# W1 kept even tiles first, weight scales and two norm roots moved from VectorE to GpSimd, and a pooling step put later, in a fused attention and MLP kernel

## The chip, the core and the metric

The kernel runs on one core of one Trainium2 chip. The metric is the device time of one execution in microseconds (us). TensorE is called PE in the profile, VectorE DVE, ScalarE ACT, GpSimd POOL, and SyncE, which issues the DMAs here, SP.

## The reference, cut to what is computed

Inputs are q, k and v of 4 batches, 8 heads, 576 positions and 64 channels, and the weights of two blocks of width 512.

```python
# attention, for each batch and head
q_d, k_d, v_d = mean over groups of 4 positions        # 144 positions
out_up    = repeat(softmax(q_d k_d^T / 8) v_d, 4)
out_local = softmax(q k^T / 8 where |i - j| < 4) v
x = out_up + out_local, heads side by side             # (4, 576, 512)
# first block
u  = x + real(fft over channels (fft over positions (x)))
un = (u - mean(u)) / sqrt(var(u) + 1e-6)               # over the 512 channels
x  = u + relu(un @ w_ch1) @ w_ch2                      # 512 -> 2048 -> 512
# second block
gate = sigmoid(causal convolution of x with 5 taps for each channel)
out  = (gate * (x @ w_val)) @ w_out
```

The weights arrive as 64-bit floats, read by the kernel as pairs of 32-bit words.

## The kernel before

**Layout.** Channels lie on the 128 partitions in 4 groups, positions along the free axis. The MLP is done in 12 units (b, j): batch b, 192 positions j. Unit (0, 0) runs in f32 with the weights as they come (`steps32`). All other units run in pairs of f16 numbers: each weight and each activation is split into a high half and a low half (`hh` and `hl`, `uh` and `ul`), and three f16 matmuls (high high, high low, low high) make a product.

**A unit on PE.** `h_group(g)`, g from 0 to 7, makes 256 of the 2048 hidden channels from W1, into one of two PSUM buffers called `ph`; ScalarE reads it out with a ReLU (`h` in the f32 unit, `hh` in the others) and, in the f16 units, VectorE makes `hl`. `c_group(g)` multiplies these by tile 8 + g of W2 into two PSUM accumulators `pc`. In the f16 units the order is h0, h1, c0, h2, c1, h3 and so on.

**The weights' way.** W1 has tiles 0 to 7 and W2 has tiles 8 to 15, each 128 x 1024.

- `load_w` brings the raw words by DMA into slots that are used several times. W2 has more tiles than slots, so a later tile's load waits until VectorE has read the earlier tile out of the slot.
- `word_w` (through `to_f32`) makes f32 numbers out of the words with three VectorE operations a tile: one tensor_scalar and two scalar_tensor_tensor of 128 x 1024.
- `sumsq_w` sums squares on PE (`gram`); `trace_w` (VectorE, then `tot` on PE) makes one number of it; `pow2` makes of this a power of two, the scale `s_w`, and its inverse, with one-column operations on VectorE.
- `conv_w` splits a tile: ScalarE writes the high half with the scale applied, VectorE the low half. The halves of a tile are written where the f32 numbers of the tile before it lay, and so the tiles are split one after another, and only when the f32 unit no longer reads what they overwrite.

Group g of `steps32` reads the even W1 tiles for g under 4 and the odd ones from there on. In the kernel before, the tiles lie and are split in the order 0, 1, 2, and so on.

**The norm.** `ln(b, j)` makes `uh` and `ul` of a unit: mean, square, sum on PE (`st`), then an inverse square root by an integer first guess and two Newton steps on tiles of 128 x 192 (`vv`, `r`), all on VectorE. For (0, 0) the root is used only at the end of the unit.

**The second batch.** Its banded attention, its pooled attention (`pool_qk` sums q and k over 4 positions into `qkT`) and its FFT run between the matmuls of the first batch's units. The value and output weights (tiles 16 to 19, `raw`) follow W2 into slots that the second batch's v gives free, and `pooled_v` on GpSimd sums v, whose loads share SP's queue with those of the weights.

**What sets the order.** The program is written as steps with positions (`put`, `spread`; constants such as `S_W1`, `S_C1`), some raised by `urgent`. A scheduler orders the instructions of each engine from these; on the chip each engine takes its instructions strictly in that order, and waits for the semaphores of each.

Of the kernel before, what the change touches and what calls it, by code (L numbers as in the profile page):

```python
# [126 lines left out]
def attn_moe_kernel(ctx, tc, q_t, k_t, v_t, w1, w2, w_val, conv_t, w_out, c_feat, c_seq, c_band, c_eye, out):  # L127
# [38 lines left out]
    def mul(eng, out, a, b):  # L166
        return eng.tensor_tensor(out=out, in0=a, in1=b, op=ALU.mult)
# [67 lines left out]

    def pow2(f2, kexp, name):

        s = keep.tile([P, 1], F32, name="s_" + name)
        iv = keep.tile([P, 1], F32, name="iv_" + name)
        c = tiny.tile([P, 1], F32, tag="p2a", name="p2a")  # L240
        V.tensor_scalar(out=c, in0=f2, scalar1=1e-30, scalar2=1e30, op0=ALU.max, op1=ALU.min)
        e = tiny.tile([P, 1], I32, tag="p2b", name="p2b")
        V.tensor_scalar(out=e, in0=c.bitcast(I32), scalar1=23, scalar2=None, op0=ALU.logical_shift_right)
        m = tiny.tile([P, 1], I32, tag="p2c", name="p2c")
        V.tensor_scalar(out=m, in0=e, scalar1=-1.0, scalar2=float(2 * kexp + 127), op0=ALU.mult, op1=ALU.add)
        h = tiny.tile([P, 1], I32, tag="p2d", name="p2d")
        V.tensor_scalar(out=h, in0=m, scalar1=1, scalar2=None, op0=ALU.arith_shift_right)
        for dst, sg in ((s, 1.0), (iv, -1.0)):
            b = tiny.tile([P, 1], I32, tag="p2e", name="p2e")
            V.tensor_scalar(out=b, in0=h, scalar1=sg, scalar2=127.0, op0=ALU.mult, op1=ALU.add)  # L250
            V.tensor_scalar(out=dst.bitcast(I32), in0=b, scalar1=23, scalar2=None, op0=ALU.logical_shift_left)
        return s, iv

    def total(cols, n, name):

        ps = pst("tot", [P, n])
        T.matmul(out=ps, lhsT=ones, rhs=cols, start=True, stop=True)
        t = keep.tile([P, 1], F32, name="f2_" + name)
# [18 lines left out]
    def hi(i):  # L277
        return halves[i].bitcast(F16)[:, 0:1024]

    def lo(i):  # L280
        return halves[i].bitcast(F16)[:, 1024:2048]

# [25 lines left out]
    def load_w(i):  # L308
        slot = SLOTS[W1_ORDER.index(i) if i < 8 else i]
# [13 lines left out]

    def word_w(i):
        if i < 16:
            raw = raws.pop(i)
            n = 1024 // len(raw)
            pos = W1_ORDER.index(i) if i < 8 else 8
            for z, x in enumerate(raw):
                last = to_f32(W[i + 1].bitcast(I32)[:, z * n:(z + 1) * n], x,  # L330
                       lambda g=gates if pos < 4 else gates1 if pos < 6 else gates2: g.pop(0) if len(g) > 1 else g[0])
            if pos == 7:
                gates2[:] = [last.ins]
                st[0]["worded"] = last
            return
# [9 lines left out]
    def sumsq_w(i, key, first, last):  # L345

        if first:
            gram[key] = pst("cv", [P, P]) if key == "wo" else ps_c.tile([P, P], F32, tag="c1", name="gram")
        x = W[i + 1].bitcast(BF16).rearrange("p (n t) -> p n t", t=2)
        for c in range(8):  # L350
# [11 lines left out]
    def trace_w(key):  # L362
        return total(diagonal(gram[key], key), 1, key)

    def conv_w(i, s, eng):

        h_, l_, r_ = hi(i), lo(i), W[i + 1]
        A.activation(out=h_, in_=r_, func=AF.Copy, scale=s[:, 0:1])
# [6 lines left out]
    def w1_scale():  # L375
        f = trace_w("w1")
        sc["f1"] = f
        sc["s1"], sc["iv1"] = pow2(f, 10, "w1")

    def w2_scale():  # L380
        f = trace_w("w2")
        sc["f2"] = f
        sc["s2"], sc["iv2"] = pow2(f, 14, "w2")
        iv12 = keep.tile([P, 1], F32, name="iv12")
# [585 lines left out]
    def ln(b, j):  # L970
# [22 lines left out]
        if head:  # L993
# [7 lines left out]
        vv = tiny.tile([P, UT], F32, tag="r2", name="vv", bufs=2)  # L1001
        V.tensor_scalar(out=vv, in0=ps, scalar1=1e-6, scalar2=None, op0=ALU.add)
        r0 = keep.tile([P, UT], F32, name="r00") if head else tiny.tile([P, UT], F32, tag="r0", name="r0", bufs=2)
        V.tensor_scalar(out=r0.bitcast(I32), in0=vv.bitcast(I32), scalar1=1, scalar2=None, op0=ALU.logical_shift_right)
        V.tensor_scalar(out=r0.bitcast(I32), in0=r0.bitcast(I32), scalar1=-1.0, scalar2=float(0x5F1FFFF9),
                        op0=ALU.mult, op1=ALU.add)
        r1 = tiny.tile([P, UT], F32, tag="r1", name="r1", bufs=2)
        for a, c in ((-0.703952253, 0.703952253 * 2.38924456), (-0.5, 1.5)):
            mul(V, r1, r0, r0)
            stt(V, r1, r1, a, vv, ALU.mult, ALU.mult)  # L1010
            stt(V, r0, r1, c, r0, ALU.add, ALU.mult)
        r1 = r0
# [30 lines left out]
    def steps32():  # L1043
# [4 lines left out]
        def h_group(g):  # L1048
# [383 lines left out]
```

## Time and profile before

| | us |
|---|---|
| median of 3 runs | 738.41 (735.47 to 739.21) |
| the profiled execution | 738.74 |
| its span, first to last instruction | 736.9 |
| PE busy in the span | 687.7 |
| DVE busy | 476.8 |
| ACT busy | 315.6 |
| POOL busy | 109.9 |

The span is the part of the execution between its first and its last instruction, and all times of the trace below count from its start. Busy time is no share of useful work: a matmul counts as busy at either level of PE's clock, which the profile gives as a granted share of full speed.

### The profile page before, as it was taken

The numbers are of one execution on the slowest core, as the hardware profiler recorded it, in microseconds if no ns is written. First come the engines' busy times: TensorE is split into PE (matmuls) and PEld (weight loads), VectorE is DVE, ScalarE is ACT, GpSimd is POOL, SyncE is SP. The second block draws the span as 40 slices with busy tenths as digits, with TensorE's granted clock in tenths as the row PEclk, the third lists the DMA queues.
The fourth block names the chain that finished last, engine by engine and source line by source line (L and its number), as shares of the span: only waits on it lengthen the run. The fifth ranks groups of instructions, "written<-read, shape, count | busy, mean of one in ns | idle before, by whom it ended". The sixth has DMA issues, their size and how long they took to land. (4 is left out here: it accounts for less than half of the span.)

```text
span 736.9 us, 18501 instructions
## 1 busy us (share of the span) xinstructions
PE 687.7 (93%) x7849; PEld 599.5 (81%) x7849; DVE 476.8 (65%) x1066; ACT 315.6 (43%) x976; POOL 109.9 (15%) x141
## 2 busy tenths in 40 slices
PE   8588799787999998899999999999999999999997
PEld 4245599676888987868898899788989989999895
DVE  4785699688897957465967823838745572642324
ACT  1674212577453536655433636654323131221213
POOL 0400000116222022420303106003010010000000
PEclk9758999996999999999999999999999999999999
DMA  9965207523323301240220001002100000000001
GB/s 237 373 224 179 87 1 265 118 81 106 117 81 102 104 2 38 66 142 3 90 88 2 16 24 42 16 2 76 38 15 16 2 11 20 2 16 1 30 2 44
DMA packets 27575, 53.02 MB, mean 72 GB/s; under 512 B 2112, under 2 KB 16320, under 8 KB 26468
## 3 DMA queue, kind: packets, MB, share of 16 engines
q1 hardware_dynamic: 27492, 51.84, 21.9%
q8 instruction: 61, 1.00, 0.6%
q14 instruction: 22, 0.18, 0.1%
HBM read 45.34 MB, written 8.26 MB: 73 GB/s over the span
## 5 line engine op out<-in xcount | busy, mean ns | idle before, releaser
L1094 PE MATMUL ph<-uh,W 128*128 128x192 f16 x1408 | 197.1, 248 | 0.0
L1094 PEld LDWEIGHTS <-W 128*128 128x128 f16 x2112 | 177.5, 99 | 5.6 <-issue 3.4
L1094 PE MATMUL ph<-ul,W 128*128 128x192 f16 x704 | 174.6, 248 | 0.2 <-DVE ul L1021 0.2
L1114 PE MATMUL pc<-hh,W 128*128 128x192 f16 x1232 | 170.7, 246 | 0.0
L1114 PEld LDWEIGHTS <-W 128*128 128x128 f16 x1848 | 153.3, 98 | 5.8 <-issue 4.3
L1114 PE MATMUL pc<-hl,W 128*128 128x192 f16 x616 | 150.9, 246 | 0.6 <-DVE hl L164 0.6
L164 DVE SCALAR_TENSOR_TENSOR hl<-ph,hh 128x384 f16<-128x384 f32 x88 | 48.4, 551 | 88.8 <-ACT hh L1098 88.8
L1098 ACT ACTIVATE hh<-ph 128x384 f16<-128x384 f32 x88 | 43.1, 490 | 94.0 <-PE ph L1094 91.1
L164 DVE SCALAR_TENSOR_TENSOR W<-X,cw,W 128x192 f32<-128x192 f32 x160 | 63.6, 453 | 1.9 <-ACT W L1169 1.7
L1206 PE MATMUL val<-yy,W 128*128 128x192 f16 x576 | 53.5, 246 | 2.5 <-DVE yy L164 1.3
L1206 PEld LDWEIGHTS <-W 128*128 128x128 f16 x576 | 47.9, 98 | 4.9 <-issue 2.9
L561 ACT ACTIVATE dP<-dS,dmx 128x64 f32<-128x64 f32 x160 | 47.9, 334 | 1.3 <-PE dPT L582 0.9
L1222 PE MATMUL out<-W,gh 128*128 128x512 f16 x144 | 45.6, 379 | 0.0
L561 ACT ACTIVATION_READ_ACCUMULATOR dP<-dS,dmx 128x1 f32 x160 | 36.5, 228 | 0.0
L711 ACT ACTIVATE E<-sc,nm 72x144 f32<-72x144 f32 x64 | 23.6, 380 | 13.7 <-PE po L747 7.1
L1114 PEld LDWEIGHTS <-Wz 128*128 128x128 f16 x264 | 23.4, 102 | 7.5 <-issue 4.0
L164 DVE SCALAR_TENSOR_TENSOR W<-W,W 128x1024 int32<-128x1024 int32 x24 | 28.6, 1216 | 0.0
L170 POOL TENSOR_TENSOR vr<-v 72x256 f32<-72x256 f32 x12 | 16.0, 1336 | 82.5 <-DMA v<-in_v_dram 79.7
L1222 PE MATMUL out<-W,gl 128*128 128x512 f16 x72 | 27.3, 379 | 0.0
L1114 PE MATMUL pc<-hh,Wz 128*128 128x192 f16 x176 | 26.4, 255 | 0.0
L1114 PE MATMUL pc<-hl,Wz 128*128 128x192 f16 x88 | 21.7, 256 | 3.6 <-DVE hl L164 3.6
L1222 PEld LDWEIGHTS <-gh 128*128 128x128 f16 x144 | 14.0, 98 | 13.5 <-issue 0.2
(241 smaller groups left out, 1213.3 us busy)
## 6 DMA issues: line engine op xcount, KB each, us to landing
W<-in_moe_w_ch_dram SPq DMA_DIRECT2D x12, 1024.0 KB
v<-in_v_dram SPq DMA_DIRECT2D x32, 144.0 KB
out_dram<-osb SPq DMA_DIRECT2D x17, 256.0 KB
vw<-in_v_dram SPq DMA_DIRECT2D x16, 256.0 KB
X<-in_q_dram SPq DMA_DIRECT2D x6, 576.0 KB
kT<-in_k_dram SPq DMA_DIRECT2D x4, 582.0 KB
X<-in_moe_w_ch_dram SPq DMA_DIRECT2D x2, 1024.0 KB
raw<-in_moe_w_ch_dram SPq DMA_DIRECT2D x4, 512.0 KB
```

Of the source, the lines that this page charges most:

```text
L164: return eng.scalar_tensor_tensor(out=out, in0=in0, scalar=scalar, in1=in1, op0=op0, op1=op1)
L170: return eng.tensor_tensor(out=out, in0=a, in1=b, op=ALU.add)
L561: A.activation(out=s_[:, z, a], in_=pss[par][:, z, a], func=AF.Exp, scale=SCALE, bias=mx[:, par, z, a:a + 1], accum_out=su[:, par, z, a:a ...
L711: A.activation(out=E[:, qc], in_=ps[:, qc], func=AF.Exp, scale=SCALE / 16, bias=nm[:, qc:qc + 1], accum_out=su[:, qc:qc + 1],)
L1094: T.matmul(out=ps[:, e], lhsT=w1_ap(pw, kc, 2 * g + e), rhs=uh[px][:, kc, :], start=(t == 0), stop=(t == 11))
L1098: A.activation(out=h_, in_=ps, func=AF.Relu)
L1114: T.matmul(out=ps[m // 2][:, m % 2], lhsT=w2_ap(pw, kk, m), rhs=x[px][:, e, :], start=(kk == 0 and (pw, px) == (0, 0) and m % 2 == 0), sto ...
L1206: T.matmul(out=ps[:, e], lhsT=wv_ap(pw, kc, 2 * mh + e), rhs=m_["y"][px][:, kc, :], start=(t == 0), stop=(t == 11))
L1222: T.matmul(out=ps, lhsT=(gh, gl)[px][:, kc, t * 128:(t + 1) * 128], rhs=wo_ap(pw, kc), start=(n == 0), stop=(n == 11))
```

## The change

It has four parts.

1. W1's tiles are kept in the order of their loads (even ones first) through a table `AT`; the first four splits have a place of their own in the program, `S_C0`, ahead of the other four.
2. `pow2` takes four operations where it took eight, everywhere; for W1 and W2 it runs on GpSimd, and their total is copied out of PSUM by ScalarE in place of two VectorE operations.
3. The roots of the norms (0, 0) and (0, 1) run on GpSimd with 9 operations each, after ScalarE has copied `vv`; the other norms keep VectorE, with one operation less.
4. `pool_qk` on the second batch's q and k waits for the words of W2 tile 11, where it waited for those of the last W1 tile.

```diff
+S_C0 = (0.24, 0.25)
+ROOT_G = ((0, 0), (0, 1))
...
-        V.tensor_scalar(out=c, in0=f2, scalar1=1e-30, scalar2=1e30, op0=ALU.max, op1=ALU.min)
+        eng.tensor_scalar(out=c, in0=f2, scalar1=1e-30, scalar2=1e30, op0=ALU.max, op1=ALU.min)
         e = tiny.tile([P, 1], I32, tag="p2b", name="p2b")
-        V.tensor_scalar(out=e, in0=c.bitcast(I32), scalar1=23, scalar2=None, op0=ALU.logical_shift_right)
-        m = tiny.tile([P, 1], I32, tag="p2c", name="p2c")
-        V.tensor_scalar(out=m, in0=e, scalar1=-1.0, scalar2=float(2 * kexp + 127), op0=ALU.mult, op1=ALU.add)
-        h = tiny.tile([P, 1], I32, tag="p2d", name="p2d")
-        V.tensor_scalar(out=h, in0=m, scalar1=1, scalar2=None, op0=ALU.arith_shift_right)
-        for dst, sg in ((s, 1.0), (iv, -1.0)):
-            b = tiny.tile([P, 1], I32, tag="p2e", name="p2e")
-            V.tensor_scalar(out=b, in0=h, scalar1=sg, scalar2=127.0, op0=ALU.mult, op1=ALU.add)
-            V.tensor_scalar(out=dst.bitcast(I32), in0=b, scalar1=23, scalar2=None, op0=ALU.logical_shift_left)
+        eng.tensor_scalar(out=e, in0=c.bitcast(I32), scalar1=-(2.0 ** -24), scalar2=kexp + 190.45, op0=ALU.mult, op1=ALU.add)
+        for dst, sg, z in ((s, 1.0, 0.0), (iv, -1.0, 254.0)):
+            eng.tensor_scalar(out=dst.bitcast(I32), in0=e, scalar1=sg * 2.0 ** 23, scalar2=z * 2.0 ** 23, op0=ALU.mult, op1=ALU.add)
...
+        if act:
+            assert n == 1
+            r = keep.tile([P, 1], F32, name="f2s_" + name)
+            A.activation(out=r, in_=ps, func=AF.Copy, scale=float(DM))
+            return r
...
+    AT = [W1_ORDER.index(i) if i < 8 else i for i in range(NPOS)]
...
-        return halves[i].bitcast(F16)[:, 0:1024]
+        return halves[AT[i]].bitcast(F16)[:, 0:1024]
...
             if pos == 7:
                 gates2[:] = [last.ins]
+            if i == 11:
                 st[0]["worded"] = last
...
-        sc["s1"], sc["iv1"] = pow2(f, 10, "w1")
+        sc["s1"], sc["iv1"] = pow2(f, 10, "w1", G)
...
-        V.tensor_scalar(out=vv, in0=ps, scalar1=1e-6, scalar2=None, op0=ALU.add)
+        e = G if (b, j) in ROOT_G else V
+        if e is G:
+            A.activation(out=vv, in_=ps, func=AF.Copy, bias=1e-6)
+        else:
+            V.tensor_scalar(out=vv, in0=ps, scalar1=1e-6, scalar2=None, op0=ALU.add)
...
-        V.tensor_scalar(out=r0.bitcast(I32), in0=vv.bitcast(I32), scalar1=1, scalar2=None, op0=ALU.logical_shift_right)
-        V.tensor_scalar(out=r0.bitcast(I32), in0=r0.bitcast(I32), scalar1=-1.0, scalar2=float(0x5F1FFFF9),
+        e.tensor_scalar(out=r0.bitcast(I32), in0=vv.bitcast(I32), scalar1=-0.5, scalar2=float(0x5F1FFFF9),
                         op0=ALU.mult, op1=ALU.add)
...
-            mul(V, r1, r0, r0)
-            stt(V, r1, r1, a, vv, ALU.mult, ALU.mult)
-            stt(V, r0, r1, c, r0, ALU.add, ALU.mult)
+            mul(e, r1, r0, r0)
+            if e is G:
+                mul(e, r1, r1, vv)
+                e.tensor_scalar(out=r1, in0=r1, scalar1=a, scalar2=c, op0=ALU.mult, op1=ALU.add)
+                mul(e, r0, r0, r1)
+            else:
+                stt(e, r1, r1, a, vv, ALU.mult, ALU.mult)
+                stt(e, r0, r1, c, r0, ALU.add, ALU.mult)
...
-    for r, f, p in ((W1_ORDER[:6], w_in, S_W1), (range(8), w_out_, S_C1), (range(8, 16), w_in2, S_W2)):
+    for r, f, p in ((W1_ORDER[:6], w_in, S_W1), (W1_ORDER[:4], w_out_, S_C0), (W1_ORDER[4:], w_out_, S_C1), (range(8, 16), w_in2, S_W2)):
```

The scheduler's order moves with it in three places that matter below.

ScalarE, at the end of the f32 unit's groups. `h` is the read-out of a group (the number is that of its buffer, one for two groups), `W_124<-W_114` the high half of the first W1 tile. Before:

```order
L1060 ACTIVATE h_1433<-ph 128x384 x2
L1060 ACTIVATE h_1486<-ph 128x384
L553 ACTIVATE dmx<-dmx 128x8
L561 ACTIVATE dP_1277,dsu<-dS,dmx 128x64 x4
L561 ACTIVATE dP_1282,dsu<-dS,dmx 128x64 x4
L1060 ACTIVATE h_1486<-ph 128x384
L1020 ACTIVATE uh<-uc 128x768
L368 ACTIVATE W_124<-W_114,s_w_1214 128x1024
```

And after the change:

```order
L1072 ACTIVATE h_1316<-ph 128x384 x2
L258 ACTIVATE f2s_w_1203<-tot 128x1
L372 ACTIVATE W_124<-W_114,s_w_1205 128x1024
L1072 ACTIVATE h_1417<-ph 128x384
L1032 ACTIVATE uh<-uc 128x768
L1072 ACTIVATE h_1417<-ph 128x384
```

The first high half stood behind all eight read-outs and now stands ahead of that of group 4; `uh` of the second unit stands ahead of that of group 5.

GpSimd, where before the change nothing stands between six small memsets and the first sum of v. After it, the last rows of 22 new ones (`r` are the roots, `p2a` to `iv_w` the scale of W1):

```order
L169 TENSOR_TENSOR r_1302<-r_1300 128x192
L169 TENSOR_TENSOR r_1302<-r_1302,vv 128x192
L244 TENSOR_SCALAR p2a<-f2s_w_1203 128x1
L1019 TENSOR_SCALAR r_1302<-r_1302 128x192
L246 TENSOR_SCALAR p2b<-p2a 128x1
L169 TENSOR_TENSOR r_1300<-r_1300,r_1302 128x192
L248 TENSOR_SCALAR s_w_1205<-p2b 128x1
L248 TENSOR_SCALAR iv_w_1206<-p2b 128x1
L172 TENSOR_TENSOR vr<-v_1819 72x256
```

The scale of W1 stands behind all nine operations of the first root and seven of the second.

VectorE, around the words of the W2 tiles 11 (`W_119<-W_122`) and 12 (`W_120<-W_123`). Before, the four poolings `qkT` stood ahead of the words of tile 8; after the change the order is:

```order
L302 TENSOR_SCALAR W_119<-W_122 128x1024
L166 SCALAR_TENSOR_TENSOR W_119<-W_122,W_119 128x1024 x2
L619 TENSOR_REDUCE qkT<-X 128x288 x4
L302 TENSOR_SCALAR W_120<-W_123 128x1024
L169 TENSOR_TENSOR uc<-uc,r_1300 128x768
L302 TENSOR_SCALAR W_120<-raw 128x512
L166 SCALAR_TENSOR_TENSOR W_124<-W_114,s_w_1205,W_124 128x1024
L554 TENSOR_REDUCE dmx<-dS 128x4 x2
L302 TENSOR_SCALAR W_120<-raw 128x512
L302 TENSOR_SCALAR W_121<-W_122 128x1024
L166 SCALAR_TENSOR_TENSOR W_120<-W_123,W_120 128x1024
```

The poolings, the norm of the second unit (`uc<-uc,r`, which waits for GpSimd) and the first low half (`W_124`) now stand in the middle of the words of tile 12. The order of SP's DMAs is the same in both kernels.

## Rows read from the trace of the kernel before

**Rows 1.** Windows: us, busy of PE, PEld, DVE, ACT, POOL, clock, DMA.

```profile
140.00:160.00 20.00, 18.81 (x254) 17.68 (x254) 16.43 (x38) 15.82 (x63) 5.90 (x5) 0.91 0.25 82
160.00:180.00 20.00, 13.74 (x143) 11.38 (x144) 17.39 (x27) 16.86 (x45) 8.24 (x4) 0.73 0.18 57
180.00:200.00 20.00, 18.62 (x173) 16.37 (x171) 15.22 (x36) 10.62 (x27) 6.77 (x8) 0.84 0.36 117
200.00:250.00 50.00, 49.31 (x542) 42.55 (x541) 44.92 (x119) 24.79 (x63) 11.12 (x10) 1.00 0.31 94
```

**Rows 2.** Timeline of PE: start, length, instructions, idle before and its releaser.

```profile
101.69 8.99 PE L1056 MATMUL ph<-u,W 128*128 128x192 f32 x54
110.52 1.46 PE L980 MATMUL st<-sq,ones 128*128 128x192 f32 x8
...
114.31 0.33 PE L257 MATMUL tot<-ss_w,ones 128*128 128x1 f32 x2
...
142.85 5.38 PE L1069 MATMUL pc<-h,W 128*128 128x192 f32 x24
...
177.34 0.32 PE L1114 MATMUL pc<-hl,Wz 128*128 128x192 f16 x1 [3.44 <-DVE hl L164]
...
198.43 0.25 PE L1114 MATMUL pc<-hh,W 128*128 128x192 f16 x1
```

**Rows 3.** Timeline of DVE while the W2 words are made.

```profile
98.90 5.13 DVE L615 TENSOR_REDUCE qkT<-X 128x288 f32<-128x1152 f32 x4
...
115.35 0.69 DVE L299 TENSOR_SCALAR W<-W 128x1024 int32<-128x1024 int32 x1 [0.64 <-DMA W<-in_moe_w_ch_dram]
115.96 0.15 DVE L259 TENSOR_REDUCE f_w<-tot 128x1 f32<-128x1 f32 x1
...
116.56 1.22 DVE L164 SCALAR_TENSOR_TENSOR W<-W,W 128x1024 int32<-128x1024 int32 x1
...
133.81 0.69 DVE L299 TENSOR_SCALAR W<-W 128x1024 int32<-128x1024 int32 x1 [2.96 <-DMA W<-in_moe_w_ch_dram]
...
135.55 0.15 DVE L251 TENSOR_SCALAR s_w<-p2e 128x1 int32<-128x1 int32 x1
```

**Rows 4.** Groups of POOL's instructions by shape: busy, mean ns, idle before.

```profile
L170 POOL TENSOR_TENSOR vr<-v 72x256 f32<-72x256 f32 x12 | 16.0, 1336 | 82.5 <-DMA v<-in_v_dram 79.7 <-PE dS L540 2.7
...
L170 POOL TENSOR_TENSOR vr<-vr,ptv 72x256 f32<-72x256 f32 x12 | 8.7, 723 | 0.9
...
L170 POOL TENSOR_TENSOR uc<-uc 128x192 f32<-128x192 f32 x6 | 3.5, 590 | 0.5
```

**Rows 5.** Timeline of POOL, one sum of v.

```profile
170.97 5.63 POOL L170 TENSOR_TENSOR vr<-v 72x256 f32<-72x256 f32 x1 [12.56 <-DMA v<-in_v_dram]
```

**Rows 6.** Timeline of DVE beside it: two convolution taps of one shape.

```profile
175.94 0.88 DVE L164 SCALAR_TENSOR_TENSOR tap<-X,cw,tap 128x192 f32<-128x192 f32 x1
...
177.21 0.41 DVE L164 SCALAR_TENSOR_TENSOR tap<-X,cw,tap 128x192 f32<-128x192 f32 x1
```

**Rows 7.** Timeline of SP's DMA queue: start of the issue, time in it.

```profile
110.16 1.50 SPq L185 DMA_DIRECT2D W<-in_moe_w_ch_dram  x2
...
119.54 6.44 SPq L185 DMA_DIRECT2D W<-in_moe_w_ch_dram  x2
...
166.53 0.35 SPq L187 DMA_DIRECT2D raw<-in_moe_w_val_dram  x1
```

**Rows 8.** Timeline of ACT: a read-out of the f32 unit, and the first high half.

```profile
116.67 0.49 ACT L1060 ACTIVATE h<-ph 128x384 f32<-128x384 f32 x1 [3.78 <-PE ph L1056]
...
135.73 1.15 ACT L368 ACTIVATE W<-W,s_w 128x1024 f16<-128x1024 f32 x1 [4.00 <-DVE s_w L251]
```

**Rows 9.** Timeline of DVE: third score group's maximum, value weights' words, `hl` of group 3.

```profile
155.22 1.28 DVE L550 TENSOR_REDUCE dmx<-dS 128x8 f32<-128x512 f32 x2
...
184.84 0.43 DVE L299 TENSOR_SCALAR W<-raw 128x512 int32<-128x512 int32 x1 [3.45 <-DMA raw<-in_moe_w_val_dram]
...
195.58 0.55 DVE L164 SCALAR_TENSOR_TENSOR hl<-ph,hh 128x384 f16<-128x384 f32 x1
```

More of the change, by code (lines that the diff above doesn't have):

```diff
@@ L233, in warm_after, with pow2 @@
                 T.matmul(out=ps, lhsT=busy[:, 0:P], rhs=busy, start=True, stop=True)
-    def pow2(f2, kexp, name):
+    def pow2(f2, kexp, name, eng=None):
+        eng = eng or V
         s = keep.tile([P, 1], F32, name="s_" + name)
@@ L240, in pow2, with total @@
         c = tiny.tile([P, 1], F32, tag="p2a", name="p2a")
-        V.tensor_scalar(out=c, in0=f2, scalar1=1e-30, scalar2=1e30, op0=ALU.max, op1=ALU.min)
+        eng.tensor_scalar(out=c, in0=f2, scalar1=1e-30, scalar2=1e30, op0=ALU.max, op1=ALU.min)
         e = tiny.tile([P, 1], I32, tag="p2b", name="p2b")
-        V.tensor_scalar(out=e, in0=c.bitcast(I32), scalar1=23, scalar2=None, op0=ALU.logical_shift_right)
-        m = tiny.tile([P, 1], I32, tag="p2c", name="p2c")
-        V.tensor_scalar(out=m, in0=e, scalar1=-1.0, scalar2=float(2 * kexp + 127), op0=ALU.mult, op1=ALU.add)
-        h = tiny.tile([P, 1], I32, tag="p2d", name="p2d")
-        V.tensor_scalar(out=h, in0=m, scalar1=1, scalar2=None, op0=ALU.arith_shift_right)
-        for dst, sg in ((s, 1.0), (iv, -1.0)):
-            b = tiny.tile([P, 1], I32, tag="p2e", name="p2e")
-            V.tensor_scalar(out=b, in0=h, scalar1=sg, scalar2=127.0, op0=ALU.mult, op1=ALU.add)
-            V.tensor_scalar(out=dst.bitcast(I32), in0=b, scalar1=23, scalar2=None, op0=ALU.logical_shift_left)
+        eng.tensor_scalar(out=e, in0=c.bitcast(I32), scalar1=-(2.0 ** -24), scalar2=kexp + 190.45, op0=ALU.mult, op1=ALU.add)
+        for dst, sg, z in ((s, 1.0, 0.0), (iv, -1.0, 254.0)):
+            eng.tensor_scalar(out=dst.bitcast(I32), in0=e, scalar1=sg * 2.0 ** 23, scalar2=z * 2.0 ** 23, op0=ALU.mult, op1=ALU.add)
         return s, iv
-    def total(cols, n, name):
+    def total(cols, n, name, act=False):
         ps = pst("tot", [P, n])
         T.matmul(out=ps, lhsT=ones, rhs=cols, start=True, stop=True)
+        if act:
[3 more added lines that the diff above has]
+            return r
         t = keep.tile([P, 1], F32, name="f2_" + name)
@@ L277, in hi @@
     def hi(i):
-        return halves[i].bitcast(F16)[:, 0:1024]
+        return halves[AT[i]].bitcast(F16)[:, 0:1024]
     def lo(i):
-        return halves[i].bitcast(F16)[:, 1024:2048]
+        return halves[AT[i]].bitcast(F16)[:, 1024:2048]
     def rows(dst, src, c, c0, n):
@@ L308, in load_w @@
     def load_w(i):
-        slot = SLOTS[W1_ORDER.index(i) if i < 8 else i]
+        slot = SLOTS[AT[i]]
         if slot is None:
@@ L327, in word_w @@
             n = 1024 // len(raw)
-            pos = W1_ORDER.index(i) if i < 8 else 8
+            pos = AT[i] if i < 8 else 8
             for z, x in enumerate(raw):
-                last = to_f32(W[i + 1].bitcast(I32)[:, z * n:(z + 1) * n], x,
+                last = to_f32(W[AT[i] + 1].bitcast(I32)[:, z * n:(z + 1) * n], x,
                        lambda g=gates if pos < 4 else gates1 if pos < 6 else gates2: g.pop(0) if len(g) > 1 else g[0])
@@ L348, in sumsq_w @@
             gram[key] = pst("cv", [P, P]) if key == "wo" else ps_c.tile([P, P], F32, tag="c1", name="gram")
-        x = W[i + 1].bitcast(BF16).rearrange("p (n t) -> p n t", t=2)
+        x = W[AT[i] + 1].bitcast(BF16).rearrange("p (n t) -> p n t", t=2)
         for c in range(8):
@@ L362, in trace_w @@
     def trace_w(key):
-        return total(diagonal(gram[key], key), 1, key)
+        return total(diagonal(gram[key], key), 1, key, key in ("w1", "w2"))
     def conv_w(i, s, eng):
-        h_, l_, r_ = hi(i), lo(i), W[i + 1]
+        h_, l_, r_ = hi(i), lo(i), W[AT[i] + 1]
         A.activation(out=h_, in_=r_, func=AF.Copy, scale=s[:, 0:1])
@@ L382, in w2_scale @@
         sc["f2"] = f
-        sc["s2"], sc["iv2"] = pow2(f, 14, "w2")
+        sc["s2"], sc["iv2"] = pow2(f, 14, "w2", G)
         iv12 = keep.tile([P, 1], F32, name="iv12")
@@ L1055, in h_group @@
                     o = (m % 8) * 128
-                    i = T.matmul(out=ps[:, e], lhsT=W[kc * 2 + m // 8 + 1][:, o:o + 128], rhs=u()[:, kc, :],
+                    i = T.matmul(out=ps[:, e], lhsT=W[AT[kc * 2 + m // 8] + 1][:, o:o + 128], rhs=u()[:, kc, :],
                                  start=(kc == 0), stop=(kc == 3))
@@ L1328, in attn_moe_kernel @@
     put(S_K, load_consts2)
-    spread([(1.0, lambda i=i: sumsq_w(i, "w1", i == 0, i == 7)) for i in range(8)], *S_G1)
+    spread([(1.0, lambda i=i: sumsq_w(i, "w1", i == W1_ORDER[0], i == W1_ORDER[7])) for i in W1_ORDER], *S_G1)
     put(S_G1[1], lambda: urgent(w1_scale, "S"))
@@ L1349, in attn_moe_kernel @@
     assert S_LD[1] <= S_T0[0] and S_L1 <= S_W1[0] and S_T0[1] <= S_S0[0] and S_S0[1] <= S_F0[0] and S_F0[1] <= S_N0
-    assert S_N0 < S_W1B <= S_W2[0] and 8 / 17 < S_C1[0] and S_C1[1] <= 9 / 17
+    assert S_N0 < S_W1B <= S_W2[0] and 4 / 17 < S_C0[0] and 8 / 17 < S_C1[0] and S_C1[1] <= 9 / 17
     assert S_S0[1] <= S_END <= S_F0[0] and 1 <= S_W3[0]
```

## The prediction, made before the changed kernel was run

> **What bounds the kernel now.** I read the windows first [rows 1]. From 200 us on PE is the bound: 49.31 of 50 us busy at a clock of 1.00, so nothing done beside it matters there. From 140 to 200 it isn't: it is busy 51.2 of 60 us, and the clock is 0.91, 0.73 and 0.84 of full, which costs (0.09 + 0.27 + 0.16) x 20 = 10.4 us more. Some 19 us are lost, and only there can this change gain much. The timelines say why: VectorE is busy 49 of these 60 us, and PE's longest wait there, 3.44 us, is for a low half that VectorE makes [rows 2]. The scale of W1 shows the queue best: its total leaves PE at 114.3, VectorE begins to read it at 115.96, and `s_w` stands at 135.55, 19.6 us for a few one-column operations of 0.15, because words of 1.22 each (1.14 from start to start) and their DMAs stand between [rows 2, 3]. The first high half follows at 135.73 [rows 8], and the f16 unit needs four split tiles.
>
> **The scale, if GpSimd had its port alone.** Up to 101.7 the PE orders agree. An f32 matmul takes 8.99/27 = 0.33 us. The new order puts the second squares' sum (1.3) after ten of them, not 27: it ends at 106.3, not 111.8 [rows 2], and ScalarE's copy of `vv` at about 106.7. The first `vv` is ready at 97.3 (my estimate from the same rows: its sum stands right ahead of the gram matmuls). An operation of 128 x 192 on GpSimd takes 0.59 [rows 4], with its gap 0.67. The first root would end at 103.3, seven operations of the second at 111.4. Four more root and scale operations and `s_w` come behind: two of 0.67 and three one-column ones, for which the trace has no row; between nothing and 0.59 I take 0.3, near the small end. That is 113.6.
>
> **It won't have it alone.** One sum of v took 5.63 us beside a busy VectorE [rows 5], while the same shape takes 0.72 [rows 4]; as it ended, a tap on VectorE took 0.88 in place of 0.41 [rows 6]. So each holds the other up, and GpSimd can lose many turns in a row. Over the run, the sum that reads two fresh tiles averages 1.34, 1.85 times the 0.72 of the other. With that factor a root operation costs 1.24: nine from 97.3 end at 108.5, seven more at 117.2, then 2 x 1.24 + 0.9 = 3.4: `s_w` at about 121. I take this. The Trainium skill ("SBUF — State Buffer", section "Who interferes with whom") says that a VectorE instruction with two SBUF inputs and a GpSimd one that reads SBUF exclude each other, and the second waits until the first finishes. By that rule alone an operation waits for about half a VectorE word, 0.57, and costs the same 1.24; the 5.63 of the row is more than one such wait, so here the measurement decides the upper end. VectorE loses too: of some 16 root operations before its poolings end, eight fall into the poolings (5.1 us [rows 3]), which read one tile. I take the other eight as holding it 0.6 each, about 4.5 us.
>
> **A wait that is new.** The high half of the first tile now stands on ScalarE ahead of the read-out of f32 group 4. Group 6 on PE needs that group's buffer. PE reaches it at 106.3 + 3.3 (ten matmuls) + 1.3 (gram, total, mask) + 5.3 (16 matmuls) + 1.7 (scores, gram) = 117.9. The read-out ends 1.15 + 0.49 after `s_w` [rows 8], at 122.6. PE stalls 4.7 us; with `s_w` at 113.6 it wouldn't.
>
> **The last W2 tile.** Taking the poolings from 98.9 puts the words of tiles 8 to 11 earlier, so tile 11's end at 112.6, not 119.4 (four words of 1.14, four halves of 0.6 and 2.0 of small work from 98.9; a load of 5.2, from 110.16 to the wait that ends at 115.35 [rows 3, 7], that now starts at 104.4; then 0.6 + 2.3). But poolings, norm and low halves now stand inside tile 12's words. With 4.5 lost they end at 132.7, where before the slot came free at 125.5, inside the issue that ends at 125.98 [rows 7]; the last load, issued there, ended VectorE's wait at 133.81 [rows 3], 8.3 later. The same from 132.7 gives 141. Then the last tile's words, with the low halves of two W1 tiles and the normalisation between them and the gram's read: 148. The second half of the f32 `pc` needs that bank; it began at 142.85 + 5.38/3 = 144.6 [rows 2]. So 3.5 us are lost here. In return 33 of 48 f16 matmuls of the first two groups (0.08 each) are done by then instead of six: 2.2 gained.
>
> **Behind it.** All W1 splits end by 155, so PE isn't short of weights again. But the scale of W2 waits for a total that stands behind nine matmuls of that second half (about 153), and three low halves of W2 now stand ahead of the third score group's maximum: 163 where it was 155.2 [rows 9], 8 later. The second batch's values and the loads of the value weights hang on it: first load at 166.5 [rows 7] + 8 + about 3 for two high halves that now precede the squares = 177.5. VectorE got the second words at 184.84 [rows 9], 18.3 after that load. In these lie the 5.63 of the blocked sum; with VectorE waiting in front of the words it would be 0.72, so 13.4: 190.9. `hl` of group 3 began 10.7 later [rows 9]; three splits and other work have gone ahead, and 4.7 remain: 195.6. Its group on PE began at 198.43 [rows 2], with time in hand; now it begins behind `hl`, at about 196.2. **Sum: 2.2 us gained**, and about 0.7 more that I take for shorter scales and norms ahead of later waits: 738.7 - 2.9 = 735.8, and 0.3 less to stand against the median, which lies that much under the profiled execution: 735.5.
>
> Nothing of this is taken back after 200 as far as the orders show: the later moves are one norm operation and four scale operations less, at places where PE is 98% busy; I cost them at nothing for that reason. Where that cover goes, they are worth up to 0.3 a unit. The early part, to 98, differs in one scale that ends long before it is read.
>
> **Rivals.**
> - *The port costs little.* GpSimd wins its turns and `s_w` is there at 113.6 to 116. No stall at group 6, VectorE 4.5 earlier, the value words with it (184 to 187), group 3 at 187.5 to 191.5. For it: the 12 sums average 1.34, not 5.6. Against it: words stand back to back here. Gain 7 to 11: 728 to 732.
> - *GpSimd starves (slower).* The place is the stretch from 97 to 122; the price is one us for each us by which `s_w` is later than about 123, where the gain of 2.2 is used up, since ScalarE's read-outs and VectorE's norm both stand behind it. At 2.0 us an operation the first root ends at 115.3, 7 more at 129.3 without the poolings' help and some 126 with it. Then 2 x 2.0 + 0.9: about 131, and 8 us late, of which about half is met while PE waits for W2 in any case: 741 to 745. A bound against worse: VectorE itself stops at `uc<-uc,r`, and from there GpSimd is alone.
> - *It changes nothing that lasts.* Value words arrive as computed or 2 us later, and the group 3 start is the old one: 737.5 to 739.
>
> **How the numbers follow.** The forecast has 0.48, the cheap port 0.22, starving 0.18, no change 0.12. A measurement of this kernel can tell 0.5% (3.7 us) from no change: faster means under 734.7. The forecast's own range, 732 to 738, is faster in about 0.2 of the 0.48; with the cheap port 0.42. Starving is slower but for its mild end, with a little of the forecast's tail: 0.18. The same: 0.40. For the range I take the low end into the cheap port (727) and the high one into starving (743).
>
> **What would show it.** Right: on GpSimd 128 x 192 operations at 1 to 1.5 us on average between 97 and 122; `s_w` near 121; PE idle of 3 to 6 us before f32 group 6, put down to ScalarE; the last W2 load later than 126; value words after 185. Wrong: `s_w` before 117, or no wait there; a clock that falls for longer after the new stall than the 10.4 us lost now; or waits of PE after 200 that grow, since the second batch's steps are shifted against it.

## The result, and the profile after

The changed kernel takes 729.99 us, median of 4 runs (727.67 to 732.15), the kernel before in the same runs 737.31: a ratio of 0.990, 95% interval 0.9857 to 0.9943. Run again later beside other kernels it gave 727.2 us and 0.9875 (0.9844 to 0.9906). The gain is 7 to 10 us, where the forecast had 2.9 (738.41 to 735.5). The profiled execution took 730.66 us, its span 728.9.

The windows of the changed kernel, in the stretches and columns of [rows 1]:

```profile
140.00:160.00 20.00, 17.80 (x198) 16.73 (x196) 18.44 (x31) 16.27 (x47) 3.06 (x6) 0.83 0.31 94
160.00:180.00 20.00, 19.33 (x279) 17.21 (x278) 15.85 (x27) 14.93 (x44) 10.46 (x9) 1.00 0.29 89
180.00:200.00 20.00, 16.54 (x171) 14.84 (x169) 17.32 (x45) 5.98 (x20) 5.47 (x6) 0.91 0.51 160
200.00:250.00 50.00, 48.63 (x556) 43.66 (x555) 40.61 (x98) 25.38 (x65) 9.05 (x13) 1.00 0.21 64
```

PE is busy 53.7 of the 60 us up to 200, where it was 51.2, at a clock of 0.83, 1.00 and 0.91 for 0.91, 0.73 and 0.84. To compare kernels I take as lost in a stretch its length less busy time multiplied by the granted clock, the last of the columns before the DMA's two; from one row for 95 to 200 us and one for 260 to 320:

```profile
95.00:200.00 105.00, 98.61 (x1091) 92.08 (x1090) 96.16 (x158) 55.62 (x169) 36.52 (x43) 0.95 0.42 129
...
260.00:320.00 60.00, 53.05 (x774) 44.50 (x773) 35.97 (x80) 35.61 (x139) 20.66 (x26) 1.00 0.18 48
```

In the change that is 105 - 98.61 x 0.95 = 11.3 us lost in the first stretch, and 60 - 53.05 = 7.0 in the second. The same two rows of the kernel before:

```profile
95.00:200.00 105.00, 92.73 (x986) 85.15 (x985) 90.45 (x178) 52.47 (x161) 20.91 (x16) 0.90 0.37 115
...
260.00:320.00 60.00, 53.41 (x781) 45.40 (x780) 35.44 (x78) 34.44 (x137) 23.16 (x28) 1.00 0.18 48
```

It lost 21.5 and 6.6. So 10 us less are lost up to 200, and nothing of it is taken back in the second stretch. The span fell by 8.0; the first 95 us, which the change hardly touches, lost 1.6 more in this execution, and 0.7 more went between 200 and 260.

The steps of the prediction, in the timelines of the changed kernel. First GpSimd, where `r` are the roots:

```profile
99.12 1.31 POOL L1012 TENSOR_SCALAR r<-vv 128x192 int32<-128x192 int32 x1 [17.63 <-ACT vv L1008]
...
101.10 3.91 POOL L169 TENSOR_TENSOR r<-r,vv 128x192 f32<-128x192 f32 x1
...
109.58 0.59 POOL L169 TENSOR_TENSOR r<-r,r 128x192 f32<-128x192 f32 x1
...
115.67 0.59 POOL L169 TENSOR_TENSOR r<-r,vv 128x192 f32<-128x192 f32 x1
...
117.66 0.19 POOL L248 TENSOR_SCALAR s_w<-p2b 128x1 int32<-128x1 int32 x1
```

The first root's nine operations stand from 99.12 to 110.17, 1.23 each. The scale stands at 117.85. In the second profile of the changed kernel the root could begin earlier, but its first operation took longer, and the scale stood at 117.92 all the same:

```profile
97.48 2.99 POOL L1012 TENSOR_SCALAR r<-vv 128x192 int32<-128x192 int32 x1 [15.95 <-ACT vv L1008]
```

VectorE in the first profile, beside [rows 3] and [rows 9]:

```profile
109.62 1.10 DVE L302 TENSOR_SCALAR W<-W 128x1024 int32<-128x1024 int32 x1
...
113.37 5.12 DVE L619 TENSOR_REDUCE qkT<-X 128x288 f32<-128x1152 f32 x4
...
119.01 0.94 DVE L169 TENSOR_TENSOR uc<-uc,r 128x768 f32<-128x768 f32 x1
...
135.23 0.68 DVE L302 TENSOR_SCALAR W<-W 128x1024 int32<-128x1024 int32 x1
...
155.48 1.28 DVE L554 TENSOR_REDUCE dmx<-dS 128x8 f32<-128x512 f32 x2
...
181.51 0.81 DVE L302 TENSOR_SCALAR W<-raw 128x512 int32<-128x512 int32 x1 [3.13 <-DMA raw<-in_moe_w_val_dram]
...
186.28 0.54 DVE L166 SCALAR_TENSOR_TENSOR hl<-ph,hh 128x384 f16<-128x384 f32 x1
```

The last W2 tile's words begin at 135.23 with no bracket behind them: VectorE no longer waits for that load (2.96 us in [rows 3]). The value weights' second words begin 3.3 us earlier than in [rows 9], and `hl` of group 3 9.3 us earlier.

### The profile page after: what moved, and what is told of

The parts are those of the page before. It is cut to its first block, busy times and chain, and to the rows that moved or that the text cites. A ratio compares the mean times of both kernels' runs of the same rounds, so it can differ in the third digit from the quotient of the medians.

```text
span 728.9 us, 18440 instructions
## 1 busy us (share of the span) xinstructions
PE 687.0 (94%) x7849; PEld 599.6 (82%) x7849; DVE 467.0 (64%) x978; ACT 316.9 (43%) x980; POOL 122.5 (17%) x167
## 4 chain that ended last, share of the span: by engine, by line
PE 67%; DVE 18%; ACT 6%; DMA 5%; POOL 2%; issue 1%; SPq 1%; POOLq 0%; ACTq 0%; DVEq 0%
PE pc L1126 19%; PE ph L1106 18%; DVE W L166 6%; PE out L1234 5%; PE val L1218 5%; ACT dP L565 3%; DMA v<-in_v_dram 2%; PE po L751 2%; PE ab L863 1%; DVE fF L835 1%; PE dO L606 1%; PE ph L1068 1%; DVE X L172 1%; PE sc L701 1%; PE pc L1081 1%
## 5 line engine op out<-in xcount | busy, mean ns | idle before, releaser
L166 DVE SCALAR_TENSOR_TENSOR W<-X,cw,W 128x192 f32<-128x192 f32 x160 | 60.2, 432 | 0.9 <-ACT W L1181 0.7
L1081 PE MATMUL pc<-h,W 128*128 128x192 f32 x128 | 26.2, 357 | 0.0
L1068 PE MATMUL ph<-u,W 128*128 128x192 f32 x128 | 24.0, 345 | 1.0 <-DVE u L996 1.0
```

What stands on the lines that cost most here:

```text
L166: return eng.scalar_tensor_tensor(out=out, in0=in0, scalar=scalar, in1=in1, op0=op0, op1=op1)
L1068: i = T.matmul(out=ps[:, e], lhsT=W[AT[kc * 2 + m // 8] + 1][:, o:o + 128], rhs=u()[:, kc, :], start=(kc == 0), stop=(kc == 3))
L1081: T.matmul(out=c["ps"][m // 2][:, m % 2], lhsT=W[9 + g][:, o:o + 128], rhs=hs[g // 2][:, g % 2, e, :], start=(kk == 0 and m % 2 == 0), sto ...
```

## The experiments

Spans are those of the profiled execution; "lost" is worked out as above from two rows of each kernel's windows; the ratios are to the kernel before in the same runs.

| kernel | span | lost 95-200 | lost 260-320 | median us | ratio, 95% interval |
|---|---|---|---|---|---|
| before | 736.9 | 21.5 | 6.6 | 737.31 | 1 |
| the change | 728.9 | 11.3 | 7.0 | 729.99 | 0.990 (0.9857 to 0.9943) |
| the change again | 724.9 | 7.6 | 6.9 | 727.2 | 0.9875 (0.9844 to 0.9906) |
| roots back on VectorE | 739.6 | 15.0 | 11.5 | 741.65 | 1.0059 (1.0038 to 1.0081) |
| scales back on VectorE | 733.3 | 7.6 | 16.1 | 735.33 | 0.9966 (0.9942 to 0.999) |
| W1's old order | 734.1 | 8.8 | 15.0 | 737.03 | 0.9992 (0.997 to 1.0015) |
| pooling at its old place | 732.2 | 10.6 | 10.1 | 735.07 | 0.9957 (0.993 to 0.9984) |
| change, scores held | 730.2 | 10.3 | 12.4 | 731.99 | 0.9939 (0.9917 to 0.996) |
| scales back, scores held | 734.7 | 7.7 | 15.5 | 735.57 | 0.9973 (0.9951 to 0.9996) |
| only the roots, scores held | 737.6 | 11.9 | 15.7 | 736.93 | 1.0002 (0.9979 to 1.0024) |
| change, longer norm | 737.4 | 8.5 | 16.1 | 739.11 | 1.0027 (1.0005 to 1.0048) |
| before, longer norm | 744.2 | 19.9 | 8.7 | 740.26 | 1.0032 (1.0006 to 1.0059) |
| change, norm's sums on PE | 726.0 | 8.5 | 4.8 | 726.78 | 0.9863 (0.9846 to 0.988) |
| scales back, norm's sums on PE | 729.2 | 8.6 | 5.7 | 727.39 | 0.9881 (0.9854 to 0.9908) |

The change itself stands there with two profiles, 11.3 and 7.6: a difference under some 4 us in a single profile's first stretch says nothing. Spans differ also by what is lost in the first 95 us, by up to 5.5.

**Four parts undone, one at a time.** My first theory (A) was that the early scale, with which splits fit between W2's words, makes the gain; the rivals were that only work taken off VectorE counts (B), and that the roots cost on the port what they save (C).

The roots:

```diff
-ROOT_G = ((0, 0), (0, 1))
+ROOT_G = ()
```

> Both early norms' roots are back on VectorE (seven operations each), everything else as in the change. Theory A (what counts is the date of the scale of W1, and with it that the first splits fit between the words of W2): GpSimd has only the scale to do, so s_w stands at 113 to 116 in place of 117.9, but VectorE carries some 5 us more before the words of W2 are done; these cost about half: 732 to 735. Theory B (the gain is the work taken off VectorE, 9.8 us of busy time): all of the roots' 5 us come back: 735 to 737. Theory C (roots beside the words on the shared port cost what they save): 728 to 730.

Measured 741.65, slower than before the change, and outside all three. The scale was early, as A has it: the first high half began at 113.84 (117.89 in the change). But VectorE took `uc<-uc,r` of the second unit, which waits for the root, only at 137.66, where the change has 119.01 and the kernel before 129.94; the root's operations stand spread between words and low halves. So the early scale isn't enough (15.0 lost up to 200), and C falls. One row of ScalarE and one of VectorE:

```profile
113.84 1.16 ACT L372 ACTIVATE W<-W,s_w 128x1024 f16<-128x1024 f32 x1 [1.48 <-POOL s_w L248]
...
137.66 0.98 DVE L169 TENSOR_TENSOR uc<-uc,r 128x768 f32<-128x768 f32 x1
```

The scales:

```diff
-        sc["s1"], sc["iv1"] = pow2(f, 10, "w1", G)
+        sc["s1"], sc["iv1"] = pow2(f, 10, "w1")
```

and the same for W2 and for the copy out of PSUM.

> The scales of W1 and W2 are back on VectorE, with the four short operations, and so are the two that bring the total out of PSUM; the roots stay on GpSimd. Theory A: the short operations stand in the queue between words, s_w comes after 126, the first splits fall behind the words, and at least half of the gain is lost: 733 to 737. Theory B: only about 1 us of work comes back to VectorE: 730 to 731.5. Theory C: 729 to 731.

Measured 735.33, as A has it, but not where A has it. The scale was late:

```profile
128.01 1.15 ACT L372 ACTIVATE W<-W,s_w 128x1024 f16<-128x1024 f32 x1 [0.99 <-DVE s_w L248]
```

Still this kernel lost only 7.6 us up to 200, no more than the change. It lost 16.1 between 260 and 320. A falls, and B (730 to 731.5) too.

The order of W1:

```diff
-    AT = [W1_ORDER.index(i) if i < 8 else i for i in range(NPOS)]
+    AT = list(range(NPOS))
...
-(W1_ORDER[:4], w_out_, S_C0), (W1_ORDER[4:], w_out_, S_C1)
+(range(8), w_out_, S_C1)
```

and with them the tiles' slots and the order in which their squares are summed.

> W1 is kept and split in the order 0, 1, 2 and so on as before the change, the rest as in the change. Theory A: the scale is early, but beyond the first two tiles a split overwrites what the f32 unit still reads, so the splits wait for its last groups; 2 to 4 us are lost: 732 to 734. Theory B: no work comes back to VectorE: 729 to 731. Theory C: as B.

Measured 737.03, beyond A's range: no gain left. Again the first stretch is as good as in the change (8.8), and the second is not (15.0).

The pooling:

```diff
             if pos == 7:
                 gates2[:] = [last.ins]
-            if i == 11:
                 st[0]["worded"] = last
```

> The second batch's q and k pooling stands ahead of the words of W2 tile 8 again, the rest as in the change. Theory A: the words of tiles 8 to 11 and the loads that wait for their slots come 5 us later, but the splits fill what would be a wait for the loads, so only 0 to 2 us are lost: 730 to 732. Theory B: no work moves between engines: 729 to 731. Theory C (the pooling is where GpSimd gets its turns): the roots have it beside their start, the scale comes earlier or at the same time: 728 to 731.

Measured 735.07, beyond A's range as well; 10.6 and 10.1 us lost. This run also shows by itself what the words beside a root cost it. The poolings now lie beside the first root, and its nine operations on GpSimd go through at their own length, from 99.35 to 104.46, where the change took 11.05 us for the same nine beside words:

```profile
99.35 0.35 POOL L1011 TENSOR_SCALAR r<-vv 128x192 int32<-128x192 int32 x1 [17.62 <-ACT vv L1007]
...
100.37 0.60 POOL L169 TENSOR_TENSOR r<-r,vv 128x192 f32<-128x192 f32 x1
...
103.87 0.59 POOL L169 TENSOR_TENSOR r<-r,r 128x192 f32<-128x192 f32 x1
```

So all kernels with the roots on GpSimd have most of the gain up to 200 (7.6 to 12 us lost, with the roots on VectorE 15, before the change 20 to 21.5); what sets them apart is the second stretch, over 100 us behind what was edited. What PE waits for there, with the scales back on VectorE (timeline of PE):

```profile
265.02 0.73 PE L990 MATMUL st<-uc,ones 128*128 128x192 f32 x2 [1.76 <-DVE uc L172]
...
267.25 0.58 PE L533 MATMUL dS<-bandb 128*128 128x512 bf16 x1 [1.50 <-ACT dP L565]
...
269.17 0.58 PE L533 MATMUL dS<-bandb 128*128 128x512 bf16 x1 [1.33 <-ACT dP L565]
...
270.72 1.01 PE L990 MATMUL st<-sq,ones 128*128 128x192 f32 x2
...
279.35 0.59 PE L533 MATMUL dS<-bandb 128*128 128x512 bf16 x1 [2.37 <-ACT dP L565]
```

The first batch's last unit has run out of matmuls at 262.6. What comes next is unit (1, 0), whose norm stands behind the second batch's FFT; band scores of the third batch (`dS`), which wait for ScalarE, stand between the norm's two sums (`st`).

**Scores held back.** The second theory (D): those scores in the norm's way are the loss. The rival (E): they are cover.

```diff
-                    behind(st[0]["ph"].ins if b == 1 and g == 0 else None, lambda: bm.append(T.matmul(
+                    behind(st[0]["ph"].ins if b == 1 and g == 0 else st[1]["normed"].ins if b == 2 else None, lambda: bm.append(T.matmul(
...
-            T.matmul(out=ps, lhsT=ones, rhs=t[:, 0], start=True, stop=True)
+            i = T.matmul(out=ps, lhsT=ones, rhs=t[:, 0], start=True, stop=True)
+            if (b, j) == (1, 0):
+                st[1]["normed"] = i
```

and `P_D[2]` moved from (2.0, 3.2) to (2.2, 3.25), so that the norm is written first. Beside it the changed kernel ran again, unaltered.

> The changed kernel once more, unaltered, so that the runs beside it can be set against it and not only against the kernel before: 728 to 732.

> The changed kernel, with the third batch's band scores held on PE until both sums of the second batch's first norm have gone; up to 265 us all engines have the order of the change. Theory D (two places: what is lost up to 200, and a second loss near 260 to 300 where these scores stand ahead of the norm's second sum): in the change only two short scores stand between the sums, so little can be won: 727 to 731. Theory E (the scores are cover for PE while the norm is made): PE waits longer, 731 to 734.

> The scales of W1 and W2 back on VectorE as in the run on the scales, and the same hold on the third batch's scores; up to 260 us all engines have the order of that run. Theory D: that run had lost only 7.7 us between 100 and 200 (idle and slow clock together), 2.9 less than the change, and then 14.1 between 260 and 300, 8.6 more; with the scores behind the norm most of the second loss goes: 726 to 730, so that the early date of the scale is not what the change lives on. Theory A (the date of the scale): still half of the gain is missing, 733 or more. Theory E: 735 or more.

> Of the change only the two roots on GpSimd and the shorter operations of norms and scales; the order of W1, the scales on VectorE and the pooling's place are those of before. The third batch's scores are held as well. Theory D: the roots' way off VectorE gives most of what is won up to 200, 6 to 10 of 10 us: 727 to 732. Theory A: without the early scale and without the new order of W1 no more than 1 to 2 us are won: 735 to 737. Theory B (only the work taken off VectorE counts): 5 to 6 us of it are the roots': 731 to 733.

The change again gave 727.2, a little under what was expected. Held scores made it slower, 731.99, in E's range, and left the kernel with the scales back where it was, 735.57 with 15.5 lost in the second stretch: D falls. The kernel with the roots alone (of the change it has these and the shorter `pow2` and norms) came to 736.93, no gain, though it lost 11.9 up to 200 in place of 21.5: what it won there it lost between 260 and 320 (15.7). The first stretch speaks for D's part on the roots, and the time against it. It is A's time, but not for A's reason. The hold alone cost the change 0.6% and the kernel with the scales back next to nothing, so whether the roots alone would be faster without it is open; that wasn't tried.

**The norm's way made longer and shorter.** The third theory (F): after the change PE reaches the end of the first batch sooner than the second batch's way (FFT, sums, root, halves) can deliver, so this way decides. The rival (G) is the prediction's first paragraph: PE is the bound there, and work beside it costs nothing. Longer:

```diff
-        for a, c in ((-0.703952253, 0.703952253 * 2.38924456), (-0.5, 1.5)):
+        for a, c in ((-0.703952253, 0.703952253 * 2.38924456), (-0.5, 1.5)) + ((-0.5, 1.5),) * (4 if (b, j) == (1, 0) else 0):
```

in the change and in the kernel before. Shorter, in the change and in the kernel with the scales back:

```diff
-LN_PE = ((0, 0), (0, 1))
+LN_PE = ((0, 0), (0, 1), (1, 0))
```

> The changed kernel with four more Newton steps, redundant ones, in the root of the second batch's first norm: 12 operations of 128 x 192 on VectorE, 0.35 to 0.36 us each alone, 4.3 us, and no other work; every engine has the order of the change up to this norm (near 271 us). Theory F (after the change the second batch's way from its FFT through this norm sets when PE can go on, near 277 us): the time grows by 3.5 to 5 us over the change, to a ratio of 0.993 to 0.997. Theory G (PE is the bound there, as the prediction has it, and what is done beside it costs nothing): no change, 0.986 to 0.991.

> The kernel before with the same four redundant steps in the same norm. Theory F: before the change 24 us of matmuls of the first batch's last unit lay beside this way, but they were used up when the halves of the new unit came; the steps cost less than in the change, 1 to 4 us: 737.5 to 741, a ratio of 1.001 to 1.006. Theory G: no change.

> The changed kernel with both sums over channels in that norm made on PE alone (four matmuls into one bank in place of two additions on VectorE and one matmul): 1.9 us less on VectorE in the way, six matmuls of 0.33, 2 us, more on PE, which is idle there for over 4 us. Theory F: 0.5 to 2 us faster than the change, a ratio of 0.984 to 0.989. Theory G: PE has 2 us more to do, so 0 to 2 us slower than the change, 0.989 to 0.993.

> The scales of W1 and W2 back on VectorE, with that norm's sums on PE as in the run beside it; with this the scheduler also sets the third batch's scores behind the norm, nearly as in the change. Theory F: that kernel's first 200 us were as good as the change's (7.7 us lost between 95 and 200 us, 10.6 in the change), and its deficit was made in this norm, so most of it goes: 727 to 731, a ratio of 0.986 to 0.992. Theory A (the early scale is what counts): 0.994 or more.

G falls. Twelve operations on VectorE, in one norm of twelve, took the whole gain: 739.11, 9 to 11 us more than the change (1.3 to 1.5%, by its two ratios). That is far over F's 3.5 to 5. VectorE's timeline of the change says what the root took there:

```profile
271.15 0.36 DVE L1010 TENSOR_SCALAR vv<-st 128x192 f32<-128x192 f32 x1 [0.75 <-PE st L990]
...
275.73 0.96 DVE L169 TENSOR_TENSOR uc<-uc,r 128x768 f32<-128x768 f32 x1
```

and with the longer norm:

```profile
269.05 0.36 DVE L1010 TENSOR_SCALAR vv<-st 128x192 f32<-128x192 f32 x1 [0.75 <-PE st L990]
...
280.43 0.96 DVE L169 TENSOR_TENSOR uc<-uc,r 128x768 f32<-128x768 f32 x1
```

It is 4.58 us in the one and 11.38 in the other, 6.8 more: 4.3 of the operations, the rest other work of VectorE that now stands between them. Then the high half had to wait for ScalarE's band work as well, and PE began the new unit 15.8 us after the norm's second sum, not 7.1. PE in the change:

```profile
270.55 0.56 PE L990 MATMUL st<-sq,ones 128*128 128x192 f32 x2 [2.49 <-DVE sq L172]
...
277.62 0.33 PE L1106 MATMUL ph<-uh,W 128*128 128x192 f16 x2 [1.63 <-ACT uh L1032]
```

and with the longer norm:

```profile
268.45 0.56 PE L990 MATMUL st<-sq,ones 128*128 128x192 f32 x2 [2.50 <-DVE sq L172]
...
284.21 0.48 PE L1106 MATMUL ph<-uh,W 128*128 128x192 f16 x2 [2.42 <-ACT uh L1032]
```

Its clock was lower as well:

```profile
260.00:320.00 60.00, 49.37 (x672) 39.98 (x670) 36.53 (x82) 32.44 (x133) 20.15 (x26) 0.89 0.17 48
```

PE was idle 10.6 us there, 3.7 more than in the change, and a mean clock of 0.89 costs 49.37 x 0.11 = 5.4. Some 1.5 of these 5.4 can't be laid to the added work: from 268 to 276 the clock was 0.68 and 0.90 (rows in the last section), and the slow matmuls end at 272.9, ahead of the first added operation at 273.62. In the kernel before the same twelve operations cost 0.3%, 2.4 us, as F has it: its way had matmuls of the first batch beside it.

With the sums on PE the change takes 726.78, in F's range; it can't be told from the change run again (the intervals overlap). The kernel with the scales back falls from 735.33 to 727.39, ratios 0.9966 and 0.9881, intervals apart: as good as the change, as F has it. In that kernel the scheduler also set most of the scores behind the norm; the run that moved these alone didn't help.

## Why the prediction came out as it did

The forecast's own time was 735.5, its own range 732 to 738. The measured 729.99 lies below that and inside the stated range (727 to 743), whose low end was taken from the first rival, the port that costs little (728 to 732). That rival's mechanism didn't come either: it had the scale at 113.6 to 116 and no stall at group 6, and the value words at 184 to 187. So that the time fell in its range is in part luck. One size of the first paragraph is too large as well: its "some 19 us" charge the low clock on idle time too; by busy time multiplied by clock the three rows lose 17.2. By the prediction's steps:

- **The roots on GpSimd.** The 1.24 us for an operation beside words came out as an average (1.23 over the first nine; 1.42 in the second profile), but through a few long waits, 3.91 and 2.99 us beside others of 0.51 to 0.59. The step that failed is the next: the factor was also laid on all of the second root and on the scale, though the same paragraph sets eight operations beside the 5.1 us of the poolings. The last six of the second root and the scale's lay there; they took 0.35 to 0.59, as in the run with the poolings first, and 0.2. So the scale came at 117.85, not 121, though the root had begun 1.8 us later than forecast. The Trainium skill ("SBUF — State Buffer", "Who interferes with whom") gives the line that I didn't draw: a VectorE instruction with at most one SBUF input, outside its 2-port modes, doesn't contend with GpSimd, and a `tensor_reduce` never does on this chip. For the reductions the trace of the change and that of the poolings first agree. The words' own one-input operation is not so clear: one took 1.10 us at 109.62, beside root operations, in place of 0.69, and in the second profile the 2.99 us lay for half their length beside such operations; whether they run in a 2-port mode no run here shows. That a GpSimd operation waits out one VectorE instruction doesn't hold here: 3.91 us at 101.10, beside words of 1.22.
- **VectorE held 4.5 us.** The mechanism is there, the size isn't: between 97 and 119 us the whole is about 1.7. VectorE's groups of that stretch by shape (count, busy, mean ns), first of the kernel before:

```profile
L164 DVE SCALAR_TENSOR_TENSOR W<-W,W 128x1024 int32<-128x1024 int32 x7 | 8.4, 1219 | 0.0
...
L164 DVE SCALAR_TENSOR_TENSOR W<-raw,W 128x512 int32<-128x512 int32 x4 | 2.6, 687 | 0.0
```

  and of the change, where two more forms (a tensor_scalar of the words and a sum of the norm) bring 0.4 each:

```profile
L166 DVE SCALAR_TENSOR_TENSOR W<-W,W 128x1024 int32<-128x1024 int32 x7 | 8.9, 1278 | 0.1
...
L166 DVE SCALAR_TENSOR_TENSOR W<-raw,W 128x512 int32<-128x512 int32 x4 | 3.1, 815 | 0.0
```

- **The new wait before f32 group 6.** It exists: 1.34 us in the second profile of the change, where PE's record has this bracket:

```profile
119.54 2.87 PE L1068 MATMUL ph<-u,W 128*128 128x192 f32 x16 [1.34 <-ACT h L1072]
```

  ScalarE there writes the first high half at 117.96 and reads group 4 out at 119.01. In the first profile it doesn't show, since PE came later by a stretch of low clock (0.63 from 92 to 96 us). It was put at 4.7; from 117.85 instead of 121 follow 3.1 less.
- **The last W2 tile.** Tile 11 ended at 113.4 (112.6 forecast) and the last load went out at 129.79 (132.7). But its data was there by 135.23, 5.4 later, where I had taken 8.3 from the load of the kernel before; in both kernels loads of v follow it in the queue within 0.5 us, and what made that one slower isn't shown. The gram was read at 142.54 and the second half of the f32 `pc` began at 142.96, not 148. These 5 us are about what lies between forecast and result.
- **Behind it.** The third scores' maximum came at 155.48 (163 forecast), the first value load at 165.91 (177.5), the second words at 181.51 (190.9), `hl` of group 3 at 186.28 (195.6). I take these 7 to 12 us as the sum of the points above, which no run separates. VectorE waits less: it is busy 96.2 of the 105 us up to 200, before 90.5.
- **"From 200 us on PE is the bound, so nothing done beside it matters there."** In the change this did no harm: after 200 it lost what the kernel before lost. As a reason it is wrong: eight kernels of the table lost 3 to 9 us more between 260 and 320 than the change, and where the norm alone was altered it was work on VectorE that PE was about to need. The prediction named that as what would make it wrong.

A rule against the change is in the Trainium skill ("GPSIMD Engine Reference", "Engine selection"): elementwise work belongs on VectorE, GpSimd being about half as fast with two inputs. By the rows a root's two-input operation takes 0.51 to 0.60 on GpSimd and 0.35 on VectorE, so the rule holds for the operation. The roots' return to VectorE cost 1.6% (11.7 us) all the same, 4 to 7 us of it up to 200: there VectorE is the engine waited for and GpSimd is not.

Open: in both profiles of the change the norm's way, from its first sum on PE to the first matmul of unit (1, 0), takes 10.85 us; with the scales back it takes 15.06, with W1's old order or the roots back 15.6, with the pooling at its old place 12.2. ScalarE's squares and high half in this norm, in the change:

```profile
268.39 0.84 ACT L1002 ACTIVATE sq<-uc 128x768 f32<-128x768 f32 x1 [5.34 <-DVE uc L996]
...
276.72 0.84 ACT L1032 ACTIVATE uh<-uc 128x768 f16<-128x768 f32 x1 [1.47 <-DVE uc L169]
```

and with the scales back:

```profile
267.95 0.87 ACT L1002 ACTIVATE sq<-uc 128x768 f32<-128x768 f32 x1
...
279.15 0.88 ACT L1032 ACTIVATE uh<-uc 128x768 f16<-128x768 f32 x1
```

In the change both start as soon as VectorE has made their input (at 268.35 and 276.69). With the scales back the input was there at 266.75 and 277.79, and the third batch's band work stood ahead of both on ScalarE, 1.2 and 1.4 us. That is 2.5 of the 4.2 us between the two kernels. No run put ScalarE's order back alone, so that the order of the scheduler makes the second loss is argued from the timelines and not shown by itself. Nor was the price of a scale later than 123 us, the second rival's, tried in the change's order; with the scales back the scale stood at 127.98, and nothing was lost by it up to 200. No run has the shorter `pow2` and norms alone. The longer norm's 9 to 11 us are accounted for to about 9 in its profile (3.7 of idle time and 5.4 of clock, with the 1.5 that the added work didn't cause).

## What to carry to other kernels

Work taken off the queue that everything waits for can be worth more than its time even on a slower engine; price its operations there by what lies beside them, instruction by instruction (two-input words double them here, one-input reductions don't). When a part is undone to find its share, look where the time is lost: three of four undone parts gave back half of the gain or all of it, over 100 us behind their edit. An engine at 98% is no proof that nothing beside it matters: follow the way of what it needs next, and see how much other work it has left to cover that way.

## What was not expected of the hardware

Idle stretches of PE of one length had different effects on its clock. In the change and with the longer norm PE takes the same matmuls in the same order up to the norm's second sum, and waits for that sum 2.49 and 2.50 us (rows above). In the change the granted clock stayed at 1.00 behind it, the level of 2.4 GHz:

```profile
268.00:272.00 4.00, 1.51 (x8) 0.86 (x8) 3.18 (x8) 3.42 (x18) 0.74 (x1) 1.00 0.00 0
272.00:276.00 4.00, 3.87 (x79) 2.37 (x78) 3.83 (x10) 1.51 (x2) 2.15 (x4) 1.00 0.17 65
```

With the longer norm it fell, before any added operation ran:

```profile
268.00:272.00 4.00, 3.55 (x11) 1.57 (x12) 3.18 (x8) 1.74 (x12) 2.29 (x4) 0.68 0.00 0
272.00:276.00 4.00, 3.45 (x75) 2.08 (x74) 3.69 (x11) 1.84 (x3) 0.59 (x1) 0.90 0.18 67
```

With the scales back PE was idle 0.73 us of the four from 260 and 2.68 of the four from 264, and the clock stood at 0.50, the level of 1.2 GHz, from 268 to 272, with PE busy again:

```profile
264.00:268.00 4.00, 1.32 (x3) 0.51 (x4) 2.59 (x6) 2.30 (x16) 0.00 (x0) 0.67 0.00 0
268.00:272.00 4.00, 2.83 (x43) 1.76 (x46) 1.29 (x5) 1.12 (x5) 1.30 (x3) 0.50 0.00 2
```

What decides whether it falls these runs don't show. So one or two of the us that a single profile loses between 260 and 320 need not be the edit's.
